# Masked attention and a two-layer product: rows without a kept key get an equal share in the turned p, and the first q and k come by two queues

## The chip, the cores and the metric

One core of a Trainium2 chip runs the kernel. The metric is the time of one execution on the device in microseconds (us), lower is better. TensorE's matmuls stand as PE in the profile and its weight loads as PEld, VectorE as DVE, ScalarE as ACT, GpSimd as POOL; SP is SyncE, which only issues transfers (DMAs). Each engine works through its own list of instructions in order and waits by semaphores for others.

## The reference

Eight batches of eight heads, 576 rows of 64 numbers each. Keys whose score lies more than `tau` under the row's largest are masked, the rest goes through a softmax and times `v`; then the heads are put side by side (4608 rows of 512) and pass two products with a leaky step between them.

```python
scores = scale * np.matmul(q, k.transpose(0, 1, 3, 2))
thresh = np.max(scores, axis=-1, keepdims=True) - tau
scores = np.where(scores >= thresh, scores, -1000000000.0)
scores = scores - np.max(scores, axis=-1, keepdims=True)
attn = np.exp(scores)
attn = attn / (np.sum(attn, axis=-1, keepdims=True) + 1e-09)
out = np.matmul(attn, v)
...
h = x @ w_in
g = np.maximum(h, 0.0) + alpha * np.minimum(h, 0.0)
return (g @ w_out).astype(np.float32)
```

A negative `tau` masks every key of a row. All its scores are then the same, so that the row's result is the mean of `v` over all 576 keys. `tau` is 0.02 in the inputs here, so that no such row occurs; both kernels have the work for it.

## The kernel before, in words

**Pairs and cycles.** Two heads are worked on as a pair, and there are 32 pairs. A pair has nine units (`UNITS`): 128 rows of one head's scores each, and one unit `"t"` that holds the last 64 rows of both. The main loop (its range begins in the last block of code) runs one cycle a unit, 288 in all. Cycle i masks unit i, computes the scores of unit i+2 and turns unit i's p; after it come its row maxima, exponents and copies. The calls are written out in this order, and PE, ACT, DVE and POOL keep it. The DMAs of SP are placed by a scheduler.

**A unit.** `scores` multiplies q, split in a high and a low part that stand in one tile `qst`, with k's parts `kh` and `kl`, into a PSUM tile `s`, of which there are two. `rowmax` (L461, DVE) reads s, `expo` (L469, ACT) writes p and the threshold `thr` (L474, ACT), and `mask` (L481, DVE) multiplies p by the comparison with `thr` and sums each row into `sm`. When `mask` has read s, its tile is free for the scores of the unit after next. `turn` and `turn_k` transpose p on PE into tiles of a PSUM pool of four, which also holds the sums of `avmul` and of the two products.

**Out of PSUM.** In the first five pairs (`whole`) the turned p is copied as it is: `hi` and `hi_k` by ACT, every fourth unit by DVE in `lo`. In the other 27 pairs it is split: `hi` rounds it (L552, ACT), and `lo` writes the rest (L556, DVE). The last 64 keys of a unit go through a tile `kw` (L573, ACT), which POOL splits. `avmul` multiplies the turned p with v. Its right-hand tiles `eo`, `rt` and `tt` carry columns of ones, so that two of a pair's four sums are 322 columns wide instead of 320, and the added columns give the sum of v over all keys.

**The end of a pair.** `recip` takes the reciprocal of `sm` plus 1e-9 (DVE), `rturn` and `rout` bring it through PE, ACT and DRAM into a tile `rb` that is broadcast over the rows of the result. `fin_add` takes the sum of v and divides it by 576 (L654, L655) and adds the two halves of the result (L658), `fin_mul` multiplies by `rb` (L664), `fin_un` (L670, DVE) writes the mean of v where the reciprocal is at least 1e8, so where no key was kept, and zero elsewhere, and `fin_out` adds that (L676, POOL; in whole pairs two halves by the helper at L76) and stores.

**Behind it.** From cycle 49 on (`FILL`, `SPC`, `RDY`) the first seven column blocks of the two products are woven into the cycles, after the last cycle the other nine follow. Weights come as 64-bit numbers and are decoded by ACT, DVE and POOL; those of the first seven blocks in cycles 0 to 48.

**The start.** `load_first` issues the transfers of pair 0's q and k, twelve, all on SP: first the 128 or 192 columns of q that the first unit of each head needs, with k between them. `prep_first_q` and `prep_first_k` make `qst`, `kh` and `kl` of them; the rest of q is treated in cycles 0 and 1 (`do(i, "mask")`, then `p.prep_first_q(i, ...)`). Pair 1's k and q are split on ACT and POOL, and then six DMAs on SP move parts of kh and kl (L385, L389) and three those of q (L411, L412, L415) to the other half of the partitions, since both heads' parts have to lie across them. Pair 1's first scores are those of cycle 7.

Of the kernel before, what the change touches and what calls it, by code (L numbers as in the profile page):

```python
# [21 lines left out]
P = 128  # L22
D = 64
# [41 lines left out]
FILL = (4, 49, 52)  # L65

# [13 lines left out]
def tile_masked_attention_moe(  # L80
# [193 lines left out]
    class Turned:  # L274


        def __init__(self, pool, dtype, parts):
# [4 lines left out]
            if parts == 1:  # L282
# [3 lines left out]
                nc.gpsimd.memset(f(self.TT[0][:, :2]), 1.0)  # L286
                nc.gpsimd.memset(f(self.TT[1][:, 320:]), 1.0)
            else:
                self.R = [[pool.tile([P, n], dtype, name=f"rt{s}{j}") for j, n in enumerate(w)] for s, w in enumerate(((256, 322), (322, 256)))]
                for j, x in ((0, self.R[1][0][:, 320:]), (1, self.R[0][1][:, :2])):  # L290
                    nc.gpsimd.memset(f(x[j * D : (j + 1) * D]), 1.0)
                    nc.gpsimd.memset(f(x[(1 - j) * D : (2 - j) * D]), 0.0)
            for i in self.parts:
                one = 1.0 - i
                nc.gpsimd.memset(f(self.EO[i][:, 0, :, 320:]), one)
                nc.gpsimd.memset(f(self.EO[i][:, 1, :, :2]), one)
# [6 lines left out]
    class Pair:  # L303
# [35 lines left out]
        def load_first(self):  # L339
            self.kr = ap1.tile([P, KW], F32, tag="vst", name=f"kr{self.pi}", bufs=2)  # L340
            qr = ap1.tile([P, 2 * S], F32, tag="p", name=f"qr{self.pi}", bufs=2)
            self.qr = qr.rearrange("p (a b) -> p a b", a=2)
            self.kh = ap1.tile([P, KW], F32R, tag="kh", name=f"kh{self.pi}", bufs=2)
            self.kl = ap1.tile([P, KW], F32R, tag="kl", name=f"kl{self.pi}", bufs=2)
            self.qst = qst_b[self.pi % 2]
            for r, src, j, (a, b) in (
                (qr, q, 0, (0, P)),
                (self.kr, k, 0, (0, S)),
                (qr, q, 1, (0, D + P)),
                (self.kr, k, 1, (0, S + D)),  # L350
                (qr, q, 0, (P, S)),
                (qr, q, 1, (D + P, S)),
            ):
                for half in range(2):
                    nc.sync.dma_start(
                        r[half * D : (half + 1) * D, j * S + a : j * S + b], src[0, 0][j * D : (j + 1) * D, a:b]
                    )

        def prep_first_k(self, j):
# [4 lines left out]
        def prep_first_q(self, j, a, b):  # L364
            qs, qr = self.qst[:, j, a:b], self.qr[:, j, a:b]
            nc.scalar.activation(qs, qr, AF.Copy, scale=0.125)
            nc.vector.scalar_tensor_tensor(qs[D:], qr[D:], 0.125, f(qs[D:]), op0=ALU.mult, op1=ALU.subtract)
# [193 lines left out]

        def hi(self, u):
            if not self.whole:
                self.put_hi(self.places(u))
            elif not EVD(9 * self.pi + u):
                self.put_whole(self.places(u), nc.scalar.copy)

        def hi_k(self, u):
            if not self.whole and UNITS[u][0] != "t":
# [3 lines left out]
                nc.scalar.copy(w, self.K[u])  # L573
# [6 lines left out]
            else:  # L580
                self.put_whole(self.places_k(u), nc.scalar.copy)

        def lo(self, u):
            if not self.whole:
                self.put_lo(self.places(u))
            elif EVD(9 * self.pi + u):
                self.put_whole(self.places(u), nc.vector.tensor_copy)
# [5 lines left out]
        def avmul(self, step, j, cs=range(5)):  # L593
# [3 lines left out]
            elif (step, j) == (0, 1):  # L597
                rhs, col, n = [t[:, 1] for t in z.EO], 0, 322
            elif (step, j) == (1, 0):
                rhs, col, n = [t[:, 0] for t in z.EO], 258, 322  # L600
# [47 lines left out]
        def fin_add(self):  # L648
            xa = self.xa
            self.vs = ap1.tile([P, 1], F32, tag="vs", name=f"vs{self.pi}", bufs=2)  # L650
            for r, c in ((slice(0, D), S + 2), (slice(D, P), 0)):
                cs = slice(c, c + 1)
                if not self.whole:
                    nc.gpsimd.tensor_tensor(xa[r, cs], xa[r, cs], self.xb[r, cs], op=ALU.add)  # L654
                nc.gpsimd.tensor_scalar(self.vs[r], xa[r, cs], 1.0 / S, None, op0=ALU.mult)  # L655
            self.x = xa[:, 2 : 2 + S]
# [9 lines left out]
        def fin_un(self):  # L666
            self.ub = self.rb
            if self.whole:
                self.ub = ap1.tile([P, S], F32, tag="ub", name=f"ub{self.pi}", bufs=1)
            nc.vector.tensor_scalar(self.ub, self.rb, 1e8, self.vs, op0=ALU.is_ge, op1=ALU.mult)  # L670

        def fin_out(self):
            if self.whole:
                halves(nc.gpsimd, self.x, self.x, self.ub, ALU.add)
            else:
                nc.gpsimd.tensor_tensor(self.x, self.x, self.rb, op=ALU.add)  # L676
# [25 lines left out]
    for p in pairs:  # L702
# [35 lines left out]
        at_cycle(o + fin[5], p.fin_un)  # L738
# [519 lines left out]
```

## Time and profile before

| | |
|---|---|
| median of 3 runs | 1364.0 us (1363.93 to 1365.26) |
| the profiled execution | 1366.29 us |
| its span, from the first instruction to the last | 1364.5 us |
| PE busy | 1326.3 us (97%) |
| DVE, ACT, POOL busy | 976.7, 837.0, 980.6 us |
| granted TensorE clock, mean | 1.000 |

The profile is of one execution. Matmuls overlap and their ends are modelled, so a PE that is busy is not a PE at its peak. An engine's idle time costs something only where PE, or what PE waits for, is held up by it. The profiled execution lies 2.3 us above the median, and its span 1.8 us under its own time.

### The profile page before, as it was taken

To read this page: it belongs to the slowest core of one execution; us is meant where nothing else is said; L and a number is where in the kernel's file an instruction comes from. 1 tells how busy PE (TensorE), PEld (TensorE's weight loads), DVE (VectorE), ACT (ScalarE), POOL (GpSimd) and SP (SyncE) were. 2 spreads that over 40 slices of the span, in tenths; PEclk is the share of its full clock that TensorE was granted. 3 is DMA by queue.
4 is the path that set the end of the run, shared out by engine and by line. 5 is a ranking of instruction groups with operands and counts; after the bars stand their busy time and mean duration, and the time that the engine had idled before them with its cause. 6 is when DMAs were issued, how large, how long until landed. Compare 5 with 4: busy or idle time off the path is not lost.

```text
span 1364.5 us, 24080 instructions
## 1 busy us (share of the span) xinstructions
PE 1326.3 (97%) x8041; PEld 1162.9 (85%) x8041; DVE 976.7 (72%) x1845; ACT 837.0 (61%) x1912; POOL 980.6 (72%) x1392
## 2 busy tenths in 40 slices
PE   5898899999999999999999999999999999999999
PEld 4565689999999999999999999988888888888887
DVE  5899888888888888889888984764665743333333
ACT  6788788888888888888888873443323322211210
POOL 2677899889889888988988975676665744433431
PEclk9999999999999999999999999999999999999999
DMA  8554454554554644554445413344556343343222
GB/s 235 150 168 120 124 156 116 155 139 118 158 148 110 168 129 128 147 143 134 131 142 148 127 53 118 101 140 156 192 170 200 125 154 123 108 139 125 93 77 85
DMA packets 113915, 186.04 MB, mean 136 GB/s; under 512 B 16672, under 2 KB 48448, under 8 KB 113792
## 3 DMA queue, kind: packets, MB, share of 16 engines
q1 hardware_dynamic: 113792, 184.51, 46.0%
q8 instruction: 64, 1.05, 0.3%
q14 instruction: 59, 0.48, 0.1%
HBM read 104.41 MB, written 37.90 MB: 104 GB/s over the span
## 4 chain that ended last, share of the span: by engine, by line
PE 82%; ACT 7%; DVE 4%; DMA 3%; POOL 2%; issue 1%; SPq 1%; POOLq 0%; ACTq 0%; DVEq 0%
PE acca L254 12%; PE pha L224 12%; PE s L446 10%; PE phc L224 9%; PE av L616 8%; PE accc L254 8%; PE accb L254 7%; PE phb L224 7%; PE t L490 7%; DVE p L481 1%; DVE nmx L461 1%; ACT p L469 1%; PE tk L506 1%; PE accc L978 1%; DMA rb<-rvd 1%
## 5 line engine op out<-in xcount | busy, mean ns | idle before, releaser
L461 DVE TENSOR_REDUCE nmx<-s 128x1 f32<-128x576 f32 x288 | 217.1, 754 | 66.7 <-PE s L446 63.8
L254 PE MATMUL acca<-wo,ga 128*128 128x512 f32 x756 | 224.3, 415 | 0.9 <-ACT xb L627 0.9
L481 DVE SCALAR_TENSOR_TENSOR p<-s,thr,p 128x576 f32<-128x576 f32 x256 | 206.8, 808 | 3.5 <-ACT thr L474 3.4
L469 ACT ACTIVATE p<-s,nmx 128x576 f32<-128x576 f32 x256 | 189.9, 742 | 17.9 <-DVE nmx L461 17.9
L446 PE MATMUL s<-kh,qst 128*128 128x288 f32 x640 | 142.5, 313 | 32.7 <-DVE p L481 13.5
L248 POOL TENSOR_TENSOR gc<-ptc,gc 128x512 fp32r<-128x512 f32 x45 | 58.2, 1293 | 144.0 <-ACT gc L245 144.0
L224 PE MATMUL pha<-xh,wi 128*128 128x256 f32 x784 | 157.8, 285 | 0.3 <-ACT pra L237 0.2
L490 PE MATMUL t<-ident,p 128*128 128x128 f32 x1024 | 155.0, 274 | 0.0
L446 PEld LDWEIGHTS s<-kh,qst 128*128 128x128 f32 x640 | 100.6, 192 | 60.5 <-issue 29.0
L254 PEld LDWEIGHTS acca<-wo,ga 128*128 128x128 f32 x756 | 133.6, 191 | 19.1 <-ACT xb L627 1.3
L245 ACT ACTIVATE gc<-ptc 128x512 fp32r<-128x512 f32 x45 | 28.4, 632 | 197.0 <-DVE ptc L948 197.0
L446 PE MATMUL s<-kl,qst 128*128 128x288 f32 x640 | 133.5, 298 | 0.0
L224 PEld LDWEIGHTS pha<-xh,wi 128*128 128x128 f32 x784 | 127.8, 190 | 6.4 <-ACT pra L237 3.5
L490 PEld LDWEIGHTS t<-ident,p 128*128 128x128 f32 x1024 | 125.2, 141 | 1.1 <-DVE e L556 0.7
L939 POOL TENSOR_TENSOR homexl<-homexr,homexh 128x512 fp32r<-128x512 f32 (+1 forms) x84 | 103.5, 1251 | 20.8 <-ACT homexh L938 20.7
L224 PE MATMUL phc<-homexh,wi 128*128 128x512 f32 x360 | 112.5, 389 | 0.0
L224 PE MATMUL pha<-xl,wi 128*128 128x256 f32 x392 | 110.7, 282 | 0.0
L577 POOL TENSOR_TENSOR rt<-kw,rt 64x128 fp32r<-64x128 f32 x216 | 97.7, 452 | 17.3
L254 PE MATMUL accc<-wo,gc 128*128 128x512 f32 x480 | 110.1, 389 | 0.0
L248 POOL TENSOR_TENSOR ga<-pta,ga 128x256 fp32r<-128x256 f32 x126 | 95.9, 763 | 18.4 <-ACT ga L245 7.8
L254 PEld LDWEIGHTS accc<-wo,gc 128*128 128x128 f32 x480 | 90.1, 188 | 18.7
L556 DVE TENSOR_TENSOR eo<-t,eo 128x512 fp32r<-128x512 f32 (+1 forms) x162 | 94.8, 599 | 12.1 <-ACT eo L552 11.0
(162 smaller groups left out, 3350.3 us busy)
## 6 DMA issues: line engine op xcount, KB each, us to landing
kr<-in_k_dram SPq DMA_DIRECT2D x31, 320.0 KB
rb<-rvd SPq DMA_DIRECT2D x64, 144.0 KB
xs<-xa SPq DMA_DIRECT2D x32, 288.0 KB
pinb<-part SPq DMA_DIRECT2D x36, 256.0 KB
part<-obb SPq DMA_DIRECT2D x36, 256.0 KB
pinc<-part SPq DMA_DIRECT2D x36, 256.0 KB
out_dram<-obc SPq DMA_DIRECT2D x35, 256.0 KB
qr<-in_q_dram SPq DMA_DIRECT2D x31, 288.0 KB
```

The costliest lines, as they stand in the source:

```text
L224: nc.tensor.matmul(ph[:, :n], w[:, c, :], xx[:, c, :n], start=(c == 0 and ti == 0), stop=(c == NCC - 1 and ti == 2),)
L248: nc.gpsimd.tensor_tensor(g[:, 1, :n], t[:, :n], f(g[:, 0, :n]), op=ALU.subtract)
L254: nc.tensor.matmul(acc[:m, :], gg[:, g, o : o + m], w, start=(first and ti == 0), stop=(last and ti == 2))
L446: nc.tensor.matmul(ps[:, h, :288], w, kk[:, a + h * 288 : a + (h + 1) * 288], start=(ki == 0 and i == 0), stop=(ki == 1 and i == n - 1),)
L461: nc.vector.tensor_reduce(self.nmx[:, j : j + 1], self.S[u][0][:, :, :288], axis=AX.XY, op=ALU.max, negate=True)
L469: nc.scalar.activation(pj, ps[:, :, :288], AF.Exp, bias=nmx[:, j : j + 1], scale=1.0)
L481: nc.vector.scalar_tensor_tensor(pj, ps[:, :, :288], thr[:, j : j + 1], pj, op0=ALU.is_ge, op1=ALU.mult, accum_out=self.sm[:, c : c + 1])
L490: nc.tensor.transpose(tb[:, c, :], pt[:, j, j * D + c * P : j * D + (c + 1) * P], ident)
L556: nc.vector.tensor_tensor(dst[1], ps, f(dst[0]), op=ALU.subtract)
L577: nc.gpsimd.tensor_tensor(lo, r, f(hi), op=ALU.subtract)
L616: nc.tensor.matmul(pa[:m, :n], w, x, start=(part == 0 and c == 0), stop=c == NKC)
L939: self.low.tensor_tensor(xl[:, c, :n], xr[:, c, :n], f(xh[:, c, :n]), op=ALU.subtract)
```

## The change

Every turned p has 1e-18 / 576 added as it leaves PSUM: ACT's copies become `Identity` with a tile `eps_sb` as bias, DVE's subtractions become one instruction that adds and subtracts, DVE's copies an addition. A row without a kept key then holds an equal share for every key. `recip` squares a row's sum where it is under one, which takes 1e-9 to 1e-18, so that the reciprocal makes the shares one 576th each; a row with a kept key has a sum of at least one and keeps it. The columns of ones, the sum of v, the comparison and the addition go, the wide sums are 320 columns, and `fin_out` follows in the cycle of `fin_un`. At the start q goes by ACT's queue in four transfers and k by SP's in four, all of q is treated ahead of the first scores, and ACT's first Exp is written behind the transfers.

```diff
-    nc.scalar.activation(ntau_sb, ident[:, :1], AF.Exp)
+    eps_sb = const.tile([P, 1], F32, name="eps_sb")
+    nc.gpsimd.memset(eps_sb, SHARE / S)
...
-            for r, src, j, (a, b) in (
-                (qr, q, 0, (0, P)),
-                (self.kr, k, 0, (0, S)),
-                (qr, q, 1, (0, D + P)),
-                (self.kr, k, 1, (0, S + D)),
-                (qr, q, 0, (P, S)),
-                (qr, q, 1, (D + P, S)),
-            ):
...
+            for eng, r, src, e in ((nc.scalar, qr, q, 0), (nc.sync, self.kr, k, D)):
+                for j in range(2):
+                    w = S + j * e
+                    for half in range(2):
+                        eng.dma_start(
+                            r[half * D : (half + 1) * D, j * S : j * S + w], src[0, 0][j * D : (j + 1) * D, :w]
+                        )
...
+            qs = self.qst[:, j, :S]
+            nc.scalar.activation(qs, self.qr[:, j], AF.Copy, scale=0.125)
+            nc.vector.scalar_tensor_tensor(qs[D:], self.qr[D:, j], 0.125, f(qs[D:]), op0=ALU.mult, op1=ALU.subtract)
             nc.scalar.activation(self.kh[:, c], self.kr[:, c], AF.Copy)
             nc.vector.tensor_tensor(self.kl[:, c], self.kr[:, c], f(self.kh[:, c]), op=ALU.subtract)
...
-                nc.scalar.activation(dst[0], ps, AF.Copy)
+                nc.scalar.activation(dst[0], ps, AF.Identity, bias=eps_sb[: ps.shape[0]])
...
-                nc.vector.tensor_tensor(dst[1], ps, f(dst[0]), op=ALU.subtract)
+                nc.vector.scalar_tensor_tensor(dst[1], ps, SHARE / S, f(dst[0]), op0=ALU.add, op1=ALU.subtract)
...
+        def copy_vec(self, out, ps):
+            nc.vector.tensor_scalar(out, ps, SHARE / S, None, op0=ALU.add)
...
-                nc.scalar.copy(w, self.K[u])
+                self.copy_act(w, self.K[u])
...
-                rhs, col, n = [t[:, 1] for t in z.EO], 0, 322
+                rhs, col, n = [t[:, 1, :, 2:] for t in z.EO], 2, 320
...
             nc.vector.tensor_scalar(self.rv, self.sm, 1e-9, None, op0=ALU.add)
+            nc.vector.scalar_tensor_tensor(self.rv, self.rv, 1.0, self.rv, op0=ALU.min, op1=ALU.mult)
             nc.vector.reciprocal(self.rv, self.rv)
...
-            nc.vector.tensor_scalar(self.ub, self.rb, 1e8, self.vs, op0=ALU.is_ge, op1=ALU.mult)
...
-                nc.gpsimd.tensor_tensor(self.x, self.x, self.rb, op=ALU.add)
...
-        at_cycle(o + fin[5], p.fin_un)
-        at_cycle(o + fin[6], p.fin_out)
+        at_cycle(o + fin[5], p.fin_out)
...
-            if i in (0, 1):
-                p.prep_first_q(i, i * D + P, S)
```

The order of the cycles' own work on PE, DVE, ACT and POOL stays; lines are shifted. The list of ACT at the program's start, before (`qr` and `kr` are q and k as they come, `p` the exponents):

```order
L105 ACT_TABLE_LOAD
L105 ACTIVATE ntau_sb<-ident 128x1
L366 ACTIVATE qst_110<-qr_178 128x128
L361 ACTIVATE kh_179<-kr_177 128x576
L366 ACTIVATE qst_110<-qr_178 128x192
L361 ACTIVATE kh_179<-kr_177 128x640
L469 ACTIVATE p_0_228<-s_0_215,nmx_0_225 128x576
```

The same place now:

```order
L340 DMA qr_167<-in_q_dram 64x576 x4
L1120 ACT_TABLE_LOAD
L1120 ACTIVATE ntau_sb<-ident 128x1
L352 ACTIVATE qst_111<-qr_167 128x576
L354 ACTIVATE kh_185<-kr_166 128x576
L352 ACTIVATE qst_111<-qr_167 128x576
L354 ACTIVATE kh_185<-kr_166 128x640
L457 ACTIVATE p_0_214<-s_0_201,nmx_0_211 128x576
```

Four issues stand ahead of the table load, and the copies of q are whole. On SP, the stretch from pair 2's k to the last move of pair 1's q, before (`wri` are weights, `kh`, `kl`, `qst` and `qt` parts of pair 1's k and q, `kr_394` and `qr_485` pair 2's k and q):

```order
L333 DMA kr_394<-in_k_dram 128x640
L385 DMA kh_249<-kh_249 64x576 x2
L126 DMA wri_401<-in_moe_w_in_dram 128x4x128
L385 DMA kl_251<-kl_251 64x576 x2
L333 DMA qr_485<-in_q_dram 128x576
L126 DMA wri_530<-in_moe_w_in_dram 128x4x128
L126 DMA wri_632<-in_moe_w_in_dram 128x4x128
L389 DMA kh_249<-kh_249 64x640
L411 DMA qst_111<-qst_111 64x576
L389 DMA kl_251<-kl_251 64x640
L412 DMA qst_111<-qt_331 64x576
L415 DMA qst_111<-qt_331 64x576
```

and now:

```order
L326 DMA kr_376<-in_k_dram 128x640
L128 DMA wri_383<-in_moe_w_in_dram 128x4x128
L326 DMA qr_467<-in_q_dram 128x576
L128 DMA wri_513<-in_moe_w_in_dram 128x4x128
L373 DMA kh_233<-kh_233 64x576 x2
L128 DMA wri_615<-in_moe_w_in_dram 128x4x128
L373 DMA kl_235<-kl_235 64x576 x2
L399 DMA qst_112<-qst_112 64x576
L400 DMA qst_112<-qt_313 64x576
L377 DMA kh_233<-kh_233 64x640
L377 DMA kl_235<-kl_235 64x640
L403 DMA qst_112<-qt_313 64x576
```

The twelve lines (with x2 counted once) hold the same transfers; the three weights and pair 2's q went ahead of moves behind which they had stood. POOL at the end of a split pair's work, before (`xa` and `xb` are the two halves of a result, `rt` and `vst` belong to the next pairs, `pta` to the products):

```order
L654 TENSOR_TENSOR xa_4314<-xa_4314,xb_4315 64x1
L655 TENSOR_SCALAR vs_4602<-xa_4314 64x1
L654 TENSOR_TENSOR xa_4314<-xa_4314,xb_4315 64x1
L655 TENSOR_SCALAR vs_4602<-xa_4314 64x1
L658 TENSOR_TENSOR xa_4314<-xa_4314,xb_4315 128x576
L576 CAST rt_120<-kw_3_4609 64x128
L577 TENSOR_TENSOR rt_120<-kw_3_4609,rt_120 64x128
```

and now:

```order
L648 TENSOR_TENSOR xa_4232<-xa_4232,xb_4233 128x576
L570 CAST rt_121<-kw_3_4521 64x128
L571 TENSOR_TENSOR rt_121<-kw_3_4521,rt_121 64x128
L570 CAST rt_122<-kw_3_4521 64x128
L571 TENSOR_TENSOR rt_122<-kw_3_4521,rt_122 64x128
```

The four one-column operations are gone, and further on the addition at L676.

## Rows read from the trace of the kernel before

**Rows 1.** Busy time of the engines in five stretches of the span: the start up to pair 1's first scores, the rest of the whole pairs, the first split pairs, the other split pairs, and what follows the last cycle. Columns: from and to, length, then for PE, PEld, DVE, ACT and POOL the busy us and in brackets the instructions, the granted clock, the busy share of the DMA engines, and GB/s.

```profile
0.00:36.60 36.60, 19.14 (x88) 14.97 (x88) 21.27 (x42) 23.17 (x51) 9.65 (x32) 1.00 0.80 223
36.60:120.00 83.40, 76.57 (x407) 49.82 (x407) 75.58 (x144) 68.19 (x156) 60.91 (x85) 1.00 0.55 155
120.00:235.00 115.00, 107.49 (x734) 92.50 (x735) 102.00 (x208) 94.65 (x228) 102.40 (x168) 1.00 0.48 131
235.00:821.00 586.00, 582.57 (x4234) 550.19 (x4234) 509.56 (x1063) 505.56 (x1208) 522.24 (x866) 1.00 0.48 133
821.00:1364.50 543.50, 540.51 (x2582) 455.38 (x2581) 268.26 (x392) 145.43 (x271) 285.36 (x244) 1.00 0.41 132
```

**Rows 2.** The chain of work that ended last, its part of the first 37 us: start, length, what (`x4`: so many in a row).

```profile
8.38 2.94 DMA tau_sb<-in_tau_dram
...
11.49 0.68 DVE nmx L461
...
15.19 1.30 PE s L446 x4
...
22.09 2.26 PE s L446 x8
...
25.82 8.49 DMA qst<-qst
...
34.33 2.31 DMA qst<-qt
...
36.89 0.77 PE s L446 x4
```

**Rows 3.** The timeline of the first 14 us, instructions in order of time: start, length, engine, line, operation, out<-in, shape; in brackets the idle time before it and what ended it.

```profile
0.73 1.28 ACT L105 ACT_TABLE_LOAD   x1 [0.73 <-PEq L1247]
0.74 1.21 SPq L355 DMA_DIRECT2D qr<-in_q_dram  x2
...
2.02 0.20 ACT L105 ACTIVATE ntau_sb<-ident 128x1 f32<-128x1 f32 x1
...
5.47 0.68 ACT L361 ACTIVATE kh<-kr 128x576 fp32r<-128x576 f32 x1 [1.67 <-DMA kr<-in_k_dram]
...
6.21 0.85 PE L446 MATMUL s<-kh,qst 128*128 128x288 f32 x2 [6.21 <-ACT kh L361]
...
13.14 0.82 DVE L481 SCALAR_TENSOR_TENSOR p<-s,thr,p 128x576 f32<-128x576 f32 x1 [0.33 <-ACT thr L474]
```

**Rows 4.** Two stretches of the start, columns as in rows 1.

```profile
0.00:12.00 12.00, 3.34 (x8) 2.00 (x8) 2.89 (x6) 3.58 (x6) 1.70 (x22) 1.00 0.48 131
12.00:32.00 20.00, 13.19 (x67) 11.40 (x67) 14.98 (x30) 15.37 (x35) 7.17 (x9) 1.00 1.08 308
```

**Rows 5.** Who waited for whom over the whole span: us in total, times, longest us.

```profile
PE s L446 <- DVE p L481: 13.5, 20, 1.2
...
PE s L446 <- DVE qst L367: 6.2, 2, 4.5
...
PE tk L506 <- ACT xb L627: 1.3, 7, 0.2
```

**Rows 6.** The same for DVE.

```profile
DVE nmx L461 <- PE s L446: 63.8, 113, 2.3
...
DVE eo L556 <- ACT eo L552: 11.0, 29, 1.0
```

**Rows 7.** Groups of instructions by line and shape: line, engine, operation, out<-in, shape, count, then busy us and mean ns of one, then idle time before.

```profile
L469 ACT ACTIVATE p<-s,nmx 128x576 f32<-128x576 f32 x256 | 189.9, 742 | 17.9 <-DVE nmx L461 17.9
L474 ACT ACTIVATE thr<-nmx,ntau_sb 128x1 f32<-128x1 f32 x288 | 85.5, 297 | 0.0
L616 PE MATMUL av<-eo,vst 128*128 128x322 f32 x432 | 75.5, 317 | 0.0
L556 DVE TENSOR_TENSOR eo<-t,eo 128x512 fp32r<-128x512 f32 x108 | 74.3, 688 | 11.3 <-ACT eo L552 11.0
L552 ACT ACTIVATE eo<-t 128x512 fp32r<-128x512 f32 x108 | 65.1, 603 | 4.6 <-PE t L490 3.8
L676 POOL TENSOR_TENSOR xa<-xa,rb 128x576 f32<-128x576 f32 x27 | 32.7, 1210 | 2.7 <-DVE rb L670 0.6
L948 DVE SCALAR_TENSOR_TENSOR ptc<-phc,ptc 128x512 f32<-128x512 f32 x45 | 31.1, 691 | 1.5
L616 PE MATMUL av<-e,vst 128*128 128x256 f32 x216 | 29.6, 280 | 0.0
L573 ACT COPY kw<-tk 128x128 f32<-128x128 f32 x108 | 28.6, 265 | 20.9 <-PE tk L506 18.5 <-POOL rt L577 0.2 <-POOL xa L654 0.2
L670 DVE TENSOR_SCALAR rb<-rb,vs 128x576 f32<-128x576 f32 x27 | 17.3, 639 | 14.4 <-POOL xa L664 14.4
L655 POOL TENSOR_SCALAR vs<-xa 64x1 f32<-64x1 f32 x64 | 13.2, 206 | 13.9 <-ACT xa L625 8.7
L632 DVE TENSOR_SCALAR rv<-sm 128x9 f32<-128x9 f32 x32 | 12.3, 384 | 0.0
L633 DVE RECIPROCAL rv<-rv 128x9 f32<-128x9 f32 x32 | 6.9, 216 | 1.1
L670 DVE TENSOR_SCALAR ub<-rb,vs 128x576 f32<-128x576 f32 x5 | 5.3, 1067 | 0.0
L362 DVE TENSOR_TENSOR kl<-kr,kh 128x576 fp32r<-128x576 f32 x1 | 0.8, 759 | 2.1 <-ACT kh L361 2.1
```

More of the change, by code (lines that the diff above doesn't have):

```diff
@@ L65 @@
 FILL = (4, 49, 52)
+SHARE = 1e-18
 def f(ap):
@@ L342, in load_first, with prep_first @@
             self.qr = qr.rearrange("p (a b) -> p a b", a=2)
-            self.kh = ap1.tile([P, KW], F32R, tag="kh", name=f"kh{self.pi}", bufs=2)
-            self.kl = ap1.tile([P, KW], F32R, tag="kl", name=f"kl{self.pi}", bufs=2)
-            self.qst = qst_b[self.pi % 2]
-            for r, src, j, (a, b) in (
-                (qr, q, 0, (0, P)),
-                (self.kr, k, 0, (0, S)),
-                (qr, q, 1, (0, D + P)),
-                (self.kr, k, 1, (0, S + D)),
-                (qr, q, 0, (P, S)),
-                (qr, q, 1, (D + P, S)),
-            ):
[L354 to L359, printed above, removed]
+            for eng, r, src, e in ((nc.scalar, qr, q, 0), (nc.sync, self.kr, k, D)):
[5 more added lines that the diff above has]
+                        )
+        def prep_first(self, j):
+            if j == 0:
+                self.kh = ap1.tile([P, KW], F32R, tag="kh", name=f"kh{self.pi}", bufs=2)
+                self.kl = ap1.tile([P, KW], F32R, tag="kl", name=f"kl{self.pi}", bufs=2)
+                self.qst = qst_b[self.pi % 2]
             c = slice(0, S) if j == 0 else slice(S, KW)
+            qs = self.qst[:, j, :S]
+            nc.scalar.activation(qs, self.qr[:, j], AF.Copy, scale=0.125)
+            nc.vector.scalar_tensor_tensor(qs[D:], self.qr[D:, j], 0.125, f(qs[D:]), op0=ALU.mult, op1=ALU.subtract)
             nc.scalar.activation(self.kh[:, c], self.kr[:, c], AF.Copy)
             nc.vector.tensor_tensor(self.kl[:, c], self.kr[:, c], f(self.kh[:, c]), op=ALU.subtract)
[L364 to L367, printed above, removed]
         def prep_kh(self):
@@ L560, in put_whole, with copy_act @@
                 copy(dst[0], ps)
+        def copy_act(self, out, ps):
+            nc.scalar.activation(out, ps, AF.Identity, bias=eps_sb[: ps.shape[0]])
+        def copy_vec(self, out, ps):
+            nc.vector.tensor_scalar(out, ps, SHARE / S, None, op0=ALU.add)
         def hi(self, u):
@@ L565, in hi @@
             elif not EVD(9 * self.pi + u):
-                self.put_whole(self.places(u), nc.scalar.copy)
+                self.put_whole(self.places(u), self.copy_act)
         def hi_k(self, u):
@@ L580, in hi_k @@
             else:
-                self.put_whole(self.places_k(u), nc.scalar.copy)
+                self.put_whole(self.places_k(u), self.copy_act)
         def lo(self, u):
@@ L597, in avmul @@
             elif (step, j) == (0, 1):
[L598 removed]
+                rhs, col, n = [t[:, 1, :, 2:] for t in z.EO], 2, 320
             elif (step, j) == (1, 0):
[L600 removed]
+                rhs, col, n = [t[:, 0, :, :320] for t in z.EO], 258, 320
             else:
@@ L603, in avmul @@
             if self.whole:
-                tr = z.TT[step][:, D + 2 :] if (step, j) == (0, 0) else z.TT[step][:, :n]
-            else:
-                tr = z.R[step][j]
+                o = D + 2 if (step, j) == (0, 0) else 2 - 2 * step
+                tr = z.TT[step][:, o : o + n]
+            else:
+                o = 2 if (step, j) == (0, 1) else 0
+                tr = z.R[step][j][:, o : o + n]
             if cs[0] == 0:
@@ L648, in fin_add @@
         def fin_add(self):
[L649 to L656, printed above, removed]
+            self.x = self.xa[:, 2 : 2 + S]
             if not self.whole:
@@ L1145, in tile_masked_attention_moe @@
         nc.sync.dma_start(alpha_sb, alpha)
-        for j in range(2):
-            p.prep_first_q(j, 0, j * D + P)
-            p.prep_first_k(j)
+        p.prep_first(0)
+        p.prep_first(1)
         nc.vector.tensor_scalar(ntau_sb, tau_sb, -1.0, None, op0=ALU.mult)
```

19 lines of the change are left out of this document (2 added, 17 removed).

## The prediction

> **What bounds the kernel now.** I read first the busy time by stage [rows 1], since the mean over the span hides that the stages differ. In each row the reader subtracts PE's busy time from the length: PE is idle 17.5 us in the start, 6.8 in the rest of the whole pairs, 7.5 in the first split pairs, 3.4 in the next 586 us and 3.0 in the last 543.5. The granted clock is 1.00 throughout. So from 235 us on PE is the bound, and an edit there gains only by giving PE less to do, or loses by making it wait. Only 31.8 us ahead of that can be gained at all.
>
> Then the chain of waits through the start [rows 2] with its timeline [rows 3], to see who releases PE there; it runs through `tau`'s transfer, the first row maximum, scores and the moves of pair 1's `qst`. Last the waits by waiter [rows 5, 6]: PE waits most for DVE's mask, 13.5 us in 20 times, and 6.2 us in two for the later parts of `qst`; DVE in turn waits 63.8 us for PE's scores, so that it has slack over the whole.
>
> **The start.** SP's first two issues take 1.21 us [rows 3], 0.6 each. Before, `tau` stands behind twelve of them, is in transit from 8.38 to 11.32, and DVE's negation of it stands ahead of the first maximum, which begins at 11.49 [rows 2]. Maximum, exponents, threshold and mask follow, the mask at 13.14 [rows 3].
>
> Now ACT issues four transfers (0.6 each, as on SP; ACT's own price isn't shown, and 0 to 1.2 are its bounds): 0.74 to 3.2. Table load 1.28, `ntau` 0.2, then q's whole copy about 0.68, as kh's copy of the same shape, to 5.4; DVE's part of it about 0.76 as `kl` [rows 7], to 6.15. The first scores began at 6.21 [rows 3] and gain nothing. But `tau` is SP's fifth transfer: issued by 3.8, plus the same transit of 2.9, landed near 6.7, so the first maximum no longer waits for it. DVE's list has the two heads' parts of q and k ahead of it, four operations of about 0.8 from 5.4 on, which puts it at about 8.65, 2.8 earlier; the mask comes 2.8 earlier as well, at 10.35. The third unit's scores, at 15.19 before, need that mask and no more q: 0.95 after the mask's start with its 0.82, so about 11.3, 3.9 earlier. The rest of q was also what held the fourth unit's scores (two waits, 6.2 us); without them my step-by-step sum puts the row at 22.09 [rows 2] at about 16.6, 5.5 earlier. The engines' order in the cycles between is unchanged, so this lead is kept to pair 1.
>
> Pair 1's first scores stand at 36.89, after the last move of its q, which lands at 36.64 [rows 2]: PE was ready 2.3 us before (34.6) [rows 5]. With the lead of 5.5 it is ready at 29.1, and if the moves are there, the gain is 36.9 - 29.1 = 7.8. Are they? The copies that feed them move forward with ACT and POOL. But the DMA engines are full from 12 to 32 us (share 1.08, 308 GB/s), and far from it in the first 12 (0.48, 131 GB/s) [rows 4]. The stage moved 223 GB/s for 36.6 us, 8.2 MB; at 308 throughout that would be 26.5 us. Three weights and pair 2's q have gone ahead of some moves on SP, so that I put the last move at 26 to 29, just in time. I take 6.5 of the 7.8; bounds 0 (all of it late) and 7.8.
>
> One rule speaks against this part. In the trace the transfers of one queue alone filled the DMA engines to a share of 1.08 [rows 4]. The Trainium skill, "DMA: Bandwidth & Descriptors", section "Issuing engines are not separate DMA queues", says that transfers started by different engines share the same 16 engines, and that starting them from several saves only the sequencer's time, usually small. The row at 131 GB/s says that in the first 12 us this sequencer time is what is short; by the rule alone the start would gain next to nothing, which is the first rival below.
>
> **PE's columns.** A wide sum of 322 columns takes 317 ns, one of 256 takes 280 [rows 7]: 0.56 ns a column. The change narrows half of a split pair's sums over its 36 steps of keys, 18 in each of 27 pairs, so 486 matmuls by two columns: 0.54 us, and some 0.16 in the whole pairs. Minus 0.7, on the bound itself. Bounds 0 and -1.
>
> **DVE.** `fin_un` goes: 27 x 0.639 + 5 x 1.067 = 22.6 us [rows 7]. `lo` turns from a subtraction into an operation with two steps; 688 ns against 691 for such an operation of the same size [rows 7], so about 1 us in all. A new small operation in `recip` is 32 x 0.216 to 0.384 (its neighbours of nine columns, rows 7), 7 to 12 us. Copies become additions, a dozen at under 0.1 each. Net some -11 us of busy time. It matters only where PE waits for masks, from 36.6 to 235 us: DVE is busy 75.6 of 83.4 and 102.0 of 115 there [rows 1]. The pairs there, about eight of 32, save a quarter of 11, 2.8 us; I take half of that on the path, -1.5. Bounds 0 and -3.5 (`fin_un` of the whole pairs falls before masks).
>
> **POOL.** The additions at L676 (32.7 us) and L655 (13.2) go, at least 46 us [rows 7]. POOL is busy 522 of 586 us in the long stage [rows 1], but PE loses only 3.4 us there to all engines together, and PE's and DVE's long waits name others [rows 5, 6]. So 0; bounds 0 and those 3.4.
>
> **ACT.** Here the change costs. All copies of turned p get a bias from a tile, 16 a split pair, 432 in 27 pairs, and 68 in the whole ones. What does the tile cost? Exponents, with a bias tile, take 742 ns for 576 columns; copies without take 603 for 512 and 265 for 128 [rows 7], thus 0.88 ns a column, 659 for 576: the difference is 83 ns. The threshold, one column with a tile, takes 297 where the copies' line gives 152 at one column: 145. I take 90, near the row that is like it in size: 500 x 0.09 = 45 us of busy time. ACT's idle time in the three cycle stages is 15.2 + 20.3 + 80.4 = 116 us [rows 1], and a split pair adds 1.4 us to a cycle group of nine in which ACT idles 3.2 or more. So ACT has room, but DVE's `lo` already waits 11.0 us in 29 times for ACT's `hi` [rows 6], and those waits grow. They are covered by DVE's own slack, the 63.8 us in which it waits for PE. If this cover were gone, 45 us would show in part (rival below). What I charge is +2: seven waits of PE for ACT's `xb` of up to 0.2 [rows 5] that become longer by 0.2 or so, and late masks in the whole pairs, where a pair has some 14 such copies. Bounds 0 and +8.
>
> **Sum.** -6.5 - 0.7 - 1.5 + 2 = -6.7. The profiled execution took 1366.3, its span 1364.5: 1359.6 for it. It lies 2.3 above the median, so the median goes from 1364.0 to 1357.3.
>
> **Rivals.**
> *The transfers hide the start.* The DMA engines being full from 12 us on, and weights standing ahead of the moves, the last move of pair 1's q lands at about 36 as before, and PE waits 7 us for it. For: the two moves took 8.49 and 2.31 us in transit [rows 2], hardly the time of their bytes but of a queue. Against: the first 12 us have room. Start 0 to -1, the rest -0.2: 1363.
>
> *ACT starts late.* If its issues cost 1.2 each, q's copy comes at 7.8 and the first scores at 8.6, so that all of the start is 2.4 late against the sum: start about -3.5 to -4, total about -4, 1360 to 1361. The table load shows 1.28, and `ntau` begins 0.01 behind it [rows 3]. The Trainium skill, "ScalarE: Activation LUTs", section "What ACT_TABLE_LOAD costs", puts about 1.38 us of drain beside the 1.28 of the load; this trace shows none. By the rule ACT would be 1.38 later and the sum -5.3.
>
> *Both gains in full.* The moves are in time (-7.8), DVE's relief ends waits for masks in full (-3.5), ACT costs nothing: -12, 1352.
>
> *ACT becomes the pace.* In the split pairs DVE's `lo` stands directly behind ACT's `hi` of the same tile, and DVE's next mask behind `lo`. If each of 8 wide copies a pair holds DVE by its 0.09, and half of the 8 narrow ones POOL and then PE, that is 27 x (0.72 + 0.36) = 29 us. With the gain of the start, 1364 - 7 + 29 = 1386; a third of it, 1367, is already slower than before. It decides from the point where DVE's 63.8 us of waits for PE don't lie in the cycles in which it needs them. For: DVE is busy 509.6 of 586 us, and waits for `hi` exist. Against: with all these waits PE idles 3.4 us in that stage, so they cost nothing yet, and DVE loses `fin_un` there.
>
> **How the numbers follow.** Forecast 0.56 with its own range 1354.5 to 1360.5; transfers hide it 0.17; ACT late 0.08; both in full 0.12; ACT the pace 0.07. What a measurement can tell from no change is 0.2%, 2.7 us: faster is under 1361.3, slower over 1366.7. Faster: nearly all of the forecast, "both", and half of "ACT late" and a little of the first rival: 0.72. Slower: "ACT the pace" and a little for what no row shows: 0.09. Same: 0.19. The range leaves out the pace's case, half of "both" and the ends: 1352 to 1364.5.
>
> **What would show it.** The start: third unit's scores at 11.3, pair 1's first at 29 to 30.5, waits of PE for `qst` from DVE gone; if pair 1's first stand at 36 behind a move, the first rival holds; if `ntau` ends after 6, the second. ACT: `hi` of 512 columns at about 690 ns, of 128 at 355, and ACT's busy time up by 45 us; under 40 ns or over 130 the term is wrong. DVE down by 11 us, POOL by 46 or more. PE's idle time from 235 to 821 us stays under 5 us, while DVE's waits for `eo` grow; if it rises by 10 or more with waits for the mask, ACT sets the pace. The forecast fails if neither the start's 36.89 moves by 4 us nor the masks' 13.5 us shrink.

## The result and the profile after

The changed kernel takes 1374.1 us (median), the kernel before in the same comparison 1364.0: ratio 1.0068, 95% interval 1.0053 to 1.0082. It is slower, and the forecast was faster. One of its four executions took 1463.4 us at a granted clock of 0.85 and is left out of the ratio. The profiled execution took 1374.02 us, its span 1372.2.

The busy time by stage, which answers to [rows 1]; columns as there.

```profile
0.00:36.60 36.60, 23.28 (x113) 18.19 (x114) 24.79 (x48) 25.39 (x53) 12.03 (x25) 0.95 0.81 232
36.60:120.00 83.40, 74.93 (x395) 49.24 (x394) 74.94 (x145) 72.31 (x157) 58.59 (x77) 0.98 0.58 166
120.00:235.00 115.00, 109.07 (x749) 94.04 (x748) 98.99 (x205) 101.72 (x232) 92.37 (x145) 1.00 0.46 125
235.00:821.00 586.00, 579.31 (x4160) 540.59 (x4160) 494.87 (x1048) 528.99 (x1195) 463.50 (x734) 1.00 0.48 132
821.00:1372.00 551.00, 547.87 (x2631) 461.67 (x2630) 270.62 (x399) 148.21 (x277) 287.49 (x247) 1.00 0.40 130
```

Read the fourth row by its counts. PE's idle time there rose from 3.4 to 6.7 us only, but PE got through 4160 matmuls in the same 586 us, where it was 4234. At 586/4234 = 0.138 us each the missing 74 are 10.2 us. Matmul ends are modelled, so a matmul that starts late stretches the busy time of the one before it; the counts don't hide that. In the first stage it is the other way round: 113 matmuls for 88, so the start did gain.

Where the lead turns into a lag is seen by following one operation that both kernels have once a cycle, DVE's maximum. Its lines in three short windows, at the first unit of pair 1, of pair 9, and at the last unit (count, duration min/median/max, first and last start). Before:

```profile
L461 DVE TENSOR_REDUCE nmx<-s x1: 758/758/758, 37.7 to 37.7; 128x1 f32<-128x576 f32 x1
...
L461 DVE TENSOR_REDUCE nmx<-s x1: 745/745/745, 238.9 to 238.9; 128x1 f32<-128x576 f32 x1
...
L461 DVE TENSOR_REDUCE nmx<-s x1: 758/758/758, 811.0 to 811.0; 128x1 f32<-128x576 f32 x1
```

and after:

```profile
L449 DVE TENSOR_REDUCE nmx<-s x1: 758/758/758, 32.7 to 32.7; 128x1 f32<-128x576 f32 x1
...
L449 DVE TENSOR_REDUCE nmx<-s x1: 757/757/757, 235.3 to 235.3; 128x1 f32<-128x576 f32 x1
...
L449 DVE TENSOR_REDUCE nmx<-s x1: 757/757/757, 817.8 to 817.8; 128x1 f32<-128x576 f32 x1
```

After is 5.0 us ahead at pair 1, 3.6 at pair 9 and 6.8 behind at the end of the cycles. So some 10.4 us go in 23 split pairs, 0.45 a pair on average. Another 1.4 go between pair 1 and pair 9, and 0.9 behind the cycles (the spans differ by 7.7).

The groups that answer to [rows 7]:

```profile
L540 ACT ACTIVATE eo<-t,eps_sb 128x512 fp32r<-128x512 f32 x108 | 74.0, 685 | 1.0 <-PE t L478 0.3
L551 ACT ACTIVATE kw<-tk,eps_sb 128x128 f32<-128x128 f32 x108 | 39.5, 366 | 17.5 <-PE tk L494 16.4
```

```profile
L544 DVE SCALAR_TENSOR_TENSOR eo<-t,eo 128x512 fp32r<-128x512 f32 x108 | 74.5, 690 | 29.8 <-ACT eo L540 28.1
L629 DVE SCALAR_TENSOR_TENSOR rv<-rv 128x9 f32<-128x9 f32 x32 | 9.5, 295 | 1.1
```

ACT's copies take 685 and 366 ns for 603 and 265, so the change costs them 82 and 101 ns (the second kind was another operation before, `COPY`). ACT's busy time rises by 39.6 us (837.0 to 876.6), DVE's falls by 12.5 and POOL's by 66.6.

The waits that answer to [rows 5, 6]:

```profile
DVE nmx L449 <- PE s L434: 65.0, 138, 1.6
...
DVE eo L544 <- ACT eo L540: 31.5, 64, 1.1
...
PE s L434 <- DVE p L469: 16.1, 22, 2.2
...
PEld pha L226 <- ACT pra L239: 10.2, 25, 0.6
...
PE tk L494 <- ACT xb L623: 1.3, 7, 0.2
```

The weight loads' wait before:

```profile
PEld pha L224 <- ACT pra L237: 3.5, 12, 0.7
```

DVE waits 31.5 us for the high halves in `eo` (11.0 before), and PE's weight loads wait 10.2 us for ACT's `pra`, a reader of the products' PSUM tiles (3.5 before). Both kernels issue the same 8041 matmuls in the same order, so that each interval between two starts can be compared. From pair 9 to the end of the cycles the intervals are 10.2 us longer in sum: 4.2 of it where a block's first `pha` follows `acca` (78 places, 291 ns on average before and 345 after), 1.9 where scores follow `av`, 1.6 where `turn` follows scores. These places take a PSUM tile that ACT or DVE must have read. The loss lies in few of them: 4024 of the 4130 intervals differ by 12 ns at most, and 52 that are longer by 0.10 to 0.34 us make 10.5 us. At 57 of the 78 `pha` places nothing is lost; 21 are 0.16 to 0.34 us later. So what PE loses is a little over two late starts a pair, each by a third of a microsecond or less.

The start, in the timeline (columns as in [rows 3]):

```profile
0.74 2.76 ACTq L340 DMA_DIRECT2D qr<-in_q_dram  x4
...
3.53 1.28 ACT L1120 ACT_TABLE_LOAD   x1 [3.53 <-issue]
...
4.83 0.20 ACT L1120 ACTIVATE ntau_sb<-ident 128x1 f32<-128x1 f32 x1
...
6.48 0.68 ACT L352 ACTIVATE qst<-qr 128x576 fp32r<-128x576 f32 x1 [1.45 <-DMA qr<-in_q_dram]
...
8.10 0.82 PE L434 MATMUL s<-kh,qst 128*128 128x288 f32 x2 [8.10 <-DVE qst L353]
...
13.46 0.82 PE L434 MATMUL s<-kh,qst 128*128 128x288 f32 x2 [1.79 <-DVE p L469]
...
18.25 0.76 PE L434 MATMUL s<-kh,qst 128*128 128x288 f32 x4 [0.63 <-DVE p L469]
...
31.89 0.54 PE L434 MATMUL s<-kh,qst 128*128 128x288 f32 x2
```

and in the chain, which names the transfer that holds it (start, length):

```profile
2.88 5.47 DMA qr<-in_q_dram
```

ACT waits 1.45 us for the first head's q; the second head's takes 5.47 us in transit and lands at 8.35. The first scores begin at 8.10, 1.9 later than before. From there on the gain builds up in the order that the prediction gave, each step smaller: the third unit's scores at 13.46 (15.19 before), the row of 22.09 at 18.25, pair 1's first scores at 31.89 (36.89 before). There PE had waited for a move:

```profile
PE s L446 <- DMA qst<-qt: 2.3, 1, 2.3
```

After the change no such wait is left.

### The profile page after: what moved, and what is told of

Its sections match the earlier page's. It is cut to its first block, busy times and chain, and to the rows that moved or that the text cites. A ratio compares the mean times of both kernels' runs of the same rounds, so it can differ in the third digit from the quotient of the medians.

```text
span 1372.2 us, 23896 instructions
## 1 busy us (share of the span) xinstructions
PE 1334.5 (97%) x8041; PEld 1163.7 (85%) x8041; DVE 964.2 (70%) x1843; ACT 876.6 (64%) x1910; POOL 914.0 (67%) x1226
## 4 chain that ended last, share of the span: by engine, by line
PE 79%; ACT 11%; DVE 7%; issue 2%; DMA 1%; POOL 1%; ACTq 0%; DVEq 0%
PE acca L256 11%; PE pha L226 11%; PE s L434 9%; PE phc L226 9%; PE accc L256 8%; PE av L612 7%; PE accb L256 7%; PE phb L226 7%; PE t L478 6%; DVE p L469 2%; DVE nmx L449 2%; ACT p L457 1%; ACT eo L540 1%; PE tk L494 1%; ACT xb L623 1%
## 5 line engine op out<-in xcount | busy, mean ns | idle before, releaser
L434 PE MATMUL s<-kh,qst 128*128 128x288 f32 x640 | 142.9, 313 | 28.4 <-DVE p L469 16.1
L226 PEld LDWEIGHTS pha<-xh,wi 128*128 128x128 f32 x784 | 127.7, 190 | 12.9 <-ACT pra L239 10.2
L544 DVE SCALAR_TENSOR_TENSOR eo<-t,eo 128x512 fp32r<-128x512 f32 (+1 forms) x162 | 94.9, 600 | 33.7 <-ACT eo L540 31.5
L250 POOL TENSOR_TENSOR ga<-pta,ga 128x256 fp32r<-128x256 f32 x126 | 95.6, 760 | 19.5 <-ACT ga L247 11.3
```

The costliest lines, as they stand in the source:

```text
L226: nc.tensor.matmul(ph[:, :n], w[:, c, :], xx[:, c, :n], start=(c == 0 and ti == 0), stop=(c == NCC - 1 and ti == 2),)
L250: nc.gpsimd.tensor_tensor(g[:, 1, :n], t[:, :n], f(g[:, 0, :n]), op=ALU.subtract)
L434: nc.tensor.matmul(ps[:, h, :288], w, kk[:, a + h * 288 : a + (h + 1) * 288], start=(ki == 0 and i == 0), stop=(ki == 1 and i == n - 1),)
L544: nc.vector.scalar_tensor_tensor(dst[1], ps, SHARE / S, f(dst[0]), op0=ALU.add, op1=ALU.subtract)
```

## The experiments

The cause is put to two theories. A: the tile operand of ACT's copies costs the cycles their 10 us and more. B: the rest of the change does it. The first four runs undo or do one part each. The runs come from several comparisons, each with the kernel before beside it (1364.0 to 1365.4 us), so that times of different comparisons agree to a microsecond or so only; the ratio is to the kernel before of the same comparison.

**The share as a number.** The changed kernel with

```diff
-                nc.scalar.activation(dst[0], ps, AF.Identity, bias=eps_sb[: ps.shape[0]])
+                nc.scalar.activation(dst[0], ps, AF.Copy, bias=SHARE / S)
...
-            nc.scalar.activation(out, ps, AF.Identity, bias=eps_sb[: ps.shape[0]])
+            nc.scalar.activation(out, ps, AF.Copy, bias=SHARE / S)
```

> The changed kernel with one edit: ACT's copies take the share as a number in the instruction (Copy with a constant bias) and not from the tile eps_sb. Theory A (the tile operand's 0.09 us on 500 ACT copies is what the cycles lose): the copies go back to about 600 and 265 ns, pair 9 to pair 31 no longer lose their 10 us against the kernel before, the start's 5 us stay: 1358 to 1362. Rival B (the loss comes from the rest of the change: DVE's two-step low halves, fin_out a cycle earlier, the longer recip): still 1370 or more, with PE's lead falling by 0.45 us a pair as now. Rival C (a number costs what a tile costs): copies still at 685 ns, 1374; it tells nothing then.

Measured 1358.1 us, ratio to before 0.9938 (0.9919 to 0.9958). The same function, with the copies back at their old price:

```profile
L540 ACT ACTIVATE eo<-t 128x512 fp32r<-128x512 f32 x108 | 64.4, 596 | 4.4 <-PE t L478 3.6
...
L551 ACT ACTIVATE kw<-tk 128x128 f32<-128x128 f32 x108 | 30.0, 277 | 20.5 <-PE tk L494 19.1 <-POOL qt L396 0.2
```

DVE's maximum at the three places, in this run:

```profile
L449 DVE TENSOR_REDUCE nmx<-s x1: 758/758/758, 32.4 to 32.4; 128x1 f32<-128x576 f32 x1
...
L449 DVE TENSOR_REDUCE nmx<-s x1: 758/758/758, 233.0 to 233.0; 128x1 f32<-128x576 f32 x1
...
L449 DVE TENSOR_REDUCE nmx<-s x1: 758/758/758, 803.2 to 803.2; 128x1 f32<-128x576 f32 x1
```

The lead over the kernel before is 5.3, 5.9 and 7.8 us: nothing is lost any more. Beside the changed kernel this run is 0.3, 2.3 and 14.6 us ahead, so the tile costs 2.3 us up to pair 9 and 12.3 in the split pairs behind it. PE's weight loads wait for `pra` as little as before:

```profile
PEld pha L226 <- ACT pra L239: 3.2, 10, 0.7
```

A holds; the tile costs 16 us here by the medians (18 by the ratios), and this version beats both kernels. Function and operand change together, from Identity with a tile to Copy with a number; no run has Identity with a number, so what is called the tile's cost is that of the two together.

**The tile alone, on the kernel before.** A bias of zeros:

```diff
+    nc.gpsimd.memset(eps_sb, 0.0)
...
-                nc.scalar.activation(dst[0], ps, AF.Copy)
+                nc.scalar.activation(dst[0], ps, AF.Identity, bias=eps_sb[: ps.shape[0]])
...
-                nc.scalar.copy(w, self.K[u])
+                self.copy_act(w, self.K[u])
```

> The kernel before with one edit: ACT's copies of turned p become Identity with a tile of zeros as bias; function and all else unchanged. Theory A: ACT +45 us busy, PE loses 10 to 14 us in the cycles, 1374 to 1379 (here fin_un is still on DVE, so rather the upper half). Rival B: 1364 to 1367.

Measured 1379.3 beside 1365.4, ratio 1.0102 (1.0086 to 1.0117): +13.9 us with nothing else changed, at the upper end of A's range. B falls. The weight loads' wait grows as in the changed kernel:

```profile
PEld pha L226 <- ACT pra L239: 10.0, 25, 0.6
```

**The start alone, on the kernel before** (the changed kernel's `load_first` and `prep_first`, Exp behind the transfers):

> The kernel before with the new start alone (q by ACT's queue and k by SP's, all of q treated first, Exp behind the transfers). Theory A: the 5 us lead at pair 1's first scores is kept to the end, 1358.5 to 1360.5. Rival D (later cycles give the lead back, whatever the bias): 1362 to 1364.

Measured 1360.8 beside 1365.4, 0.9963 (0.9948 to 0.9977). This is 0.3 over A's range and 1.2 under D's. In the profile the lead is 5.3 us at pair 1 and 5.9 at the last unit, so the start is worth 4.6 us and they are kept. Which part of the start gives them (the second queue, fewer transfers, q treated whole) wasn't tried.

**The changed kernel with the old start:**

> The changed kernel with the start of the kernel before. Theory A, in which start and cycles add: 1378 to 1380. Rival D (the lead of the start is given back in the cycles anyway): 1374 to 1376. If the lower granted clock around 25 to 30 us belongs to the new start, it is 1.00 here.

Measured 1377.8, ratio to before 1.0087 (1.0072 to 1.0102), 3.7 above the changed kernel: between the two ranges, nearer A's. In the profiles it is behind the changed kernel by 3.5 us at pair 1 and 4.0 at the last unit, so the start's gain isn't given back. The first 120 us are at a granted clock of 1.00 here, so the fall of the changed kernel's clock between 20 and 30 us comes with the new start. The other fall, behind the 0.98 of the second row, doesn't: the changed kernel has it in 115 to 120 us (0.66), this run in 120 to 125 (0.66). Its cause wasn't tried. What is left of the change without start and tile is the run with the number less the start alone, 1358.1 - 1360.8 = -2.7; their intervals overlap.

The next question is why added ACT time makes PE wait at all, where ACT idled 116 us in the cycles: by which copies (A1: all ACT time alike; A2: only those of the `kw` chain), and whether a copy's latency or ACT's queue is what counts.

**High halves plain** (DVE's low halves then carry the share):

```diff
-                nc.scalar.activation(dst[0], ps, AF.Identity, bias=eps_sb[: ps.shape[0]])
+                nc.scalar.activation(dst[0], ps, AF.Copy)
```

> The changed kernel with ACT's high halves copied plainly again (Copy without bias, 324 copies); DVE's low halves still add the share, so that high and low together hold it. Copies of kw and those of the whole pairs keep the tile. Theory A1 (each us of ACT work put in costs PE the same, some 0.35 us): ACT -29 us, time -10: 1363 to 1365. Rival A2 (only the narrow chain kw to POOL to PE counts, the wide copies are covered by DVE's slack): 1371 to 1374.

Measured 1362.8.

**`kw` plain:**

```diff
-                self.copy_act(w, self.K[u])
+                nc.scalar.activation(w, self.K[u], AF.Copy)
```

> The changed kernel with ACT's 108 copies of kw without bias; the share is left out for the last 64 keys of a unit. Theory A1: ACT -11 us, time -3 to -5: 1369 to 1371. Rival A2: 1360 to 1363. Rival A3 (kw has slack of its own, since ACT waits for PE there): 1373 to 1374.

Measured 1368.4. Both kinds count, each 0.2 to 0.6 us under A1's range; A2 and A3 fall. A1's one price doesn't hold to the letter: `kw` plain saves 5.7 us for 7.3 us of ACT's busy time, the high halves 11.3 for 25.1, so 0.8 and 0.45 us a us.

**ACT time that nobody waits for**, on the run with the number:

```diff
             do(i, "hi")
+            if 0 <= i < total:
+                nc.scalar.activation(spare, ident[:, :1], AF.Copy)
```

> The run with the share as a number, and in each of the 288 cycles one more ACT operation of one column, behind the cycle's copies, that nobody waits for (some 0.16 to 0.2 us, 45 to 58 us of ACT time in all, as much as the tiles took). Theory A1 (ACT's queue: any ACT time in the cycles costs PE about 0.35 to 0.4 us a us): 1374 to 1380. Rival G (only a copy that PE or DVE waits for costs; time behind the copies fills ACT's idle time): 1358 to 1362.

Measured 1364.9, 6.8 more than without, in neither range. The 288 operations are shown with 57.5 us, but overlap their neighbours: ACT's busy time rises by 21.6 (837.7 to 859.3), less than either theory had reckoned with. Per us of ACT it is 0.31, near A1's price, where G has none. So G falls: ACT's queue counts, not a copy's latency alone. PE's weight loads wait longer for `pra`, the next cycle's, which stands behind these operations in ACT's list (3.2 us without them):

```profile
PEld pha L227 <- ACT pra L240: 5.8, 21, 0.6
```

In the stage of the split pairs:

```profile
235.00:821.00 586.00, 582.19 (x4210) 547.24 (x4209) 493.12 (x1053) 518.45 (x1411) 469.50 (x746) 1.00 0.47 132
```

PE has 4210 matmuls there, between the 4230 of the run with the number and the 4160 of the changed kernel.

**The threshold left out**, on the run with the number, to see whether less ACT work would go on gaining (this kernel masks by another rule and serves only to take work from ACT):

```diff
-                nc.scalar.activation(self.S[u][2][:, c], nmx[:, c], AF.Identity, bias=ntau_sb, scale=-1.0)
...
-                pj, ps[:, :, :288], thr[:, j : j + 1], pj, op0=ALU.is_ge, op1=ALU.mult, accum_out=self.sm[:, c : c + 1]
+                pj, ps[:, :, :288], ntau_sb, pj, op0=ALU.is_ge, op1=ALU.mult, accum_out=self.sm[:, c : c + 1]
```

> The run with the share as a number, with the threshold left out: ACT's 288 operations of 0.3 us go (some 75 to 85 us), and the mask compares the scores with one column that is the same for all rows. Theory A1 going on below the load of that run (0.33 us a us of ACT, as the four runs between 837.7 and 876.6 us of ACT show): it would give 25 us, but PE's own work is a floor, so 1340 to 1352. Rival H (the slope begins at the load of the kernel before, where ACT's room is just used up): 1355 to 1358.

Measured 1352.9: 5.2 us for 48.8 us of ACT, between the two theories.

```profile
235.00:821.00 586.00, 584.57 (x4250) 553.05 (x4250) 493.79 (x1057) 468.09 (x998) 471.53 (x746) 1.00 0.48 134
```

Six kernels with the new start that differ by ACT's work (ACT's busy time from each page, time the median, ratio to the kernel before of its comparison):

| kernel | ACT busy, us | time, us | ratio |
|---|---|---|---|
| number, threshold left out | 788.9 | 1352.9 | 0.9911 |
| number | 837.7 | 1358.1 | 0.9938 |
| high halves plain | 851.5 | 1362.8 | 0.9981 |
| number and spare operations | 859.3 | 1364.9 | 0.9997 |
| `kw` plain | 869.3 | 1368.4 | 1.0022 |
| the changed kernel | 876.6 | 1374.1 | 1.0068 |

It is 0.11 us a us from the first row to the second, where ACT's load is that of the kernel before (837.0), and 0.41 on average above. One kernel on the lower side doesn't show where the price changes, nor whether it falls there because ACT has room or because PE itself has little left to gain: in the stage of the split pairs PE idles 1.4 us without the threshold.

**The threshold by POOL**, in the run with the number and in the changed kernel:

```diff
-THR = 'a'
+THR = "p"
```

> The run with the share as a number, with the threshold of cycles 52 on computed by POOL, not ACT (236 operations of 0.3 us off ACT, 70 us; POOL gets 236 of about 0.2). Theory A1, going on below: PE idles little in this run, so it can gain 3 to 8 us at most: 1350 to 1355. Rival H (at this load ACT's time is covered, the slope of 0.35 begins above it): 1357 to 1359. Rival I (the threshold is late behind POOL's long operations, so the mask is): 1362 to 1375.

> The changed kernel itself, tiles and all, with the threshold of cycles 52 on by POOL: ACT has about 70 us less from 135 us on. Theory A1: the cycles no longer lose 0.45 us a pair, 1358 to 1364. Rival G2 (the tiles cost by the latency of the copies alone, not by ACT's queue): 1370 or more. Rival I as in the run beside it: whatever that run loses against the run with the number is lost here too.

Measured 1409.0 and 1414.6. Rival I, and dearer than its range: the threshold stands behind POOL's long operations, and DVE's mask waits for it. From the first of the two, a wait and the group:

```profile
DVE p L469 <- POOL thr L460: 46.3, 53, 3.1
```

```profile
L460 POOL TENSOR_SCALAR thr<-nmx,tau_sb 128x1 f32<-128x1 f32 x236 | 68.5, 292 | 23.2 <-DVE nmx L449 11.0 <-DMA rb<-rvd 1.5
```

ACT is relieved by 42 us and it doesn't help, since the mask is late. So these two runs don't decide between A1 and G2 or H. Only their difference tells something of the tiles: with the masks as the bound they cost 5.6 us, not 16.

**The gap and the clock.** The run with the number, and more filler in cycle 3:

```diff
+            if i == 3:
+                filler.run(7)
```

> The run with the share as a number, and seven more filler matmuls (14 instructions, about 1.9 us of PE) in cycle 3, in the gap of PE of about 2 us that ends at 23.7 us. If the lower granted clock near 25 to 30 us follows that gap, it is 1.00 here and the time 1 to 1.5 us under the run with the number alone; if it does not, the clock still falls and the time is the same or 1 us longer.

Measured 1356.8, beside 1358.1 without; the runs of the two overlap (1355.4 to 1357.6, 1356.0 to 1359.3), so the gain isn't settled. For the clock look at 20 to 25 and 25 to 30 us, before:

```profile
20.00:25.00 5.00, 4.39 (x20) 3.99 (x19) 3.49 (x8) 3.60 (x8) 0.54 (x1) 1.00 1.09 288
25.00:30.00 5.00, 3.77 (x27) 3.36 (x27) 4.88 (x11) 4.71 (x13) 2.94 (x5) 1.00 1.08 281
```

the changed kernel:

```profile
20.00:25.00 5.00, 2.63 (x17) 2.45 (x18) 5.00 (x11) 4.76 (x10) 2.44 (x3) 0.93 1.10 298
25.00:30.00 5.00, 5.00 (x26) 4.08 (x25) 4.01 (x9) 3.86 (x10) 3.80 (x6) 0.73 0.73 175
```

and with the filler:

```profile
20.00:25.00 5.00, 4.64 (x39) 4.36 (x38) 5.00 (x11) 4.61 (x13) 3.24 (x5) 1.00 1.09 302
25.00:30.00 5.00, 4.75 (x27) 3.04 (x26) 5.00 (x10) 4.42 (x11) 2.94 (x4) 1.00 0.77 175
```

After the gap, in which PE was busy 2.63 of 5 us, the granted clock falls to a mean of 0.73, so to the lower of its two levels for part of the stretch; with the gap filled it stays at 1.00, and pair 1 comes 0.7 us earlier in the profiled execution. All four executions with the filler have a mean clock of 1.000, those with the number alone 0.997 to 1.000. So the fall goes with the gap, but not each time: with the threshold left out PE was busy 3.23 us in 20 to 25 us, and the profile shows 1.00 in both stretches.

**A third start**, on the run with the number: ACT's queue takes only the first units' columns of q, the rest goes by SP behind `tau` and is treated in cycles 0 and 1.

```diff
-            for eng, r, src, e in ((nc.scalar, qr, q, 0), (nc.sync, self.kr, k, D)):
...
+            self.first(
+                (nc.scalar, qr, q, 0, (0, P)),
+                (nc.sync, self.kr, k, 0, (0, S)),
+                (nc.scalar, qr, q, 1, (0, D + P)),
+                (nc.sync, self.kr, k, 1, (0, S + D)),
+            )
...
+            self.first((nc.sync, qr, q, 0, (P, S)), (nc.sync, qr, q, 1, (D + P, S)))
```

> The run with the share as a number, and a third start: ACT's queue takes only the columns of q that the first units need (four transfers), SP's k, tau and then the rest of q; the rest is treated in cycles 0 and 1 as before. Theory E (in the new start the first scores are held by 1.2 MB that eight transfers move at once at 217 GB/s; fewer bytes come sooner): first scores at 6.2 or earlier, pair 1's first scores 1 to 2.5 us before those of the run with the number, time 1355.5 to 1357. Rival F (the later parts of q are late again): 1358 to 1360.

Measured 1360.1. The first scores come at 6.12 (7.74 in the run with the number), as E had it, but then F holds:

```profile
12.26 0.82 PE L444 MATMUL s<-kh,qst 128*128 128x288 f32 x2 [3.02 <-DVE qst L365]
...
33.37 0.50 PE L444 MATMUL s<-kh,qst 128*128 128x288 f32 x2 [1.50 <-DMA qst<-qt]
```

PE waits 3.0 us for the rest of q, and pair 1 waits for a move again.

## Why the prediction was wrong

- **ACT, +2 with bounds 0 and +8: the step that failed.** The price of the tile was right (taken 0.09, measured 0.08 to 0.10; ACT's busy time +45 taken, +39.6 shown). The Trainium skill ("ScalarE: Activation LUTs", section "What ACT_TABLE_LOAD costs") gives about 93 ns for such an operand; the copies with the tile and with a number differ by 89 here, in both sizes. What failed is "They are covered by DVE's own slack, the 63.8 us in which it waits for PE": on that ground the waits that the copies cause in the split pairs were charged nothing, and the +2 was laid on seven waits for `xb` and on the whole pairs. The seven waits stayed at 1.3 us in sum, the stretch up to pair 9 cost 2.3, and the split pairs behind it 12.3. In all the tile cost 13.9 us on the kernel before and 16 on the changed one. DVE's waits for PE are 65.0 after, as large as ever, while PE loses 10 us: slack of one engine at some moments covers nothing at others. ACT's idle 116 us were the same kind of sum. ACT works in order, and 16 copies a pair push back everything behind them, `pra` among it, which no term had priced: PE's weight loads wait for it 3.2 to 3.5 us without the tile and 10.0 to 10.2 with it.
- **The rival "ACT becomes the pace"** had the right engine and sign, at a chance of 0.07; its price of 29 us and its third were on either side of what was measured. Its path and its condition went through DVE's masks and slack. PE's waits for masks only went from 13.5 to 16.1 us, while the largest part of the loss stands where `pha` follows `acca`, and a run shows that ACT's own queue counts. Its argument against, that PE idles only 3.4 us in that stage, read the modelled busy time as if it showed every late start (without the threshold, PE gains 5.3 us on the kernel before from pair 9 to the last unit); the sign that PE's idle time would stay under 5 us failed by little, with 6.7, for the same reason.
- **The start, -6.5: right in kind, too large.** Measured -4.6 alone. The first scores were to stay at 6.2 and began at 8.10, and the first maximum, forecast for 8.65, began at 10.75: the sum had q in SBUF when ACT was ready for it, but with eight whole transfers at once (DMA share of the first 10 us 0.81, 0.43 before) ACT waited for it, and the last of q landed at 8.35. The moves were in time, so that the rival "the transfers hide the start" falls for this start (it shows in the third one).
- **"ACT starts late"** falls by its own sign, since `ntau` ends at 5.03 and not after 6: four issues took 2.76 us, 0.69 each, near what was taken, and `ntau` began 0.02 behind the table load's end (3.53 + 1.28 = 4.81). The late first scores that it priced came all the same, from q's transit. The 1.38 us of drain that the same section of the Trainium skill puts beside the load doesn't show here either.
- **The clock** stood in no term. It fell in most profiles in which PE had the gap that the earlier start opened; what that costs isn't settled.
- **PE's columns and DVE, -0.7 and -1.5**: -2.7 measured for these and POOL together, within the noise of the two runs that it is taken from. `av` of the wide form goes from 75.5 to 75.0 us; the new step of `recip` takes 9.5, within 7 to 12; what POOL's 66.6 us less are worth no run shows by itself.

Put together, -4.6 - 2.7 + 16 = 8.7. This sum tests nothing: each term is one run less the run before it, so it must give the changed kernel's 1374.1 less the 1365.4 that the kernel before took in that comparison. With the tile's cost as measured on the kernel before it is -4.6 - 2.7 + 13.9 = 6.6, beside 10.1 in the changed kernel's own comparison, and the 2 to 3.5 us between aren't resolved. Which of the short waits carries how much of the tile's cost was read from the intervals and the waits and not tried one by one.

## What to carry to other kernels

A small constant on a PSUM copy belongs in the instruction as a number, where that form exists: here Identity with a tile of it cost 0.09 us a copy and 16 us in all, while copies with a number took what plain ones take, within some 12 ns. An engine's idle time summed over a stage is no cover for work added in many small pieces; ask where its queue ends late in each cycle, and price the added time at a share (here 0.3 to 0.8, by what waited behind it) and not at zero. Where busy times are modelled, compare how many matmuls pass in the same stretch, not the idle time.

## What was not expected

The first operation of `recip`, whose work is unchanged, went from 384 to 216 ns (32 times) when a second small one was put behind it. A one-column ACT operation is shown with 200 ns, but 288 of them added 21.6 us to ACT's busy time, 75 ns each. The threshold's 288 operations, 85.6 us by their row, freed only 48.8: of 200 and 297 ns some 125 lay within the neighbours' time in both cases.
